# Linear attention and a gated MLP in one kernel: other transposes for two output pairs, other PSUM banks in the tail, other engine orders

## The chip, the cores and the metric

One core of one Trainium2 chip. The metric is the device time of one launch in microseconds (us). TensorE is called PE here, VectorE DVE, ScalarE ACT, GpSimd POOL, SyncE SP.

## The reference

```python
h  = x + A(layernorm(x))          # x: 1 x 2048 x 448, bf16
h2 = h + B(layernorm(h))          # the output

def A(x):                         # linear attention, 16 heads of 28
    q, k, v = split(x @ wqkv)     # wqkv: 448 x 1344
    phi = lambda t: where(t > 0, t + 1, exp(t)) + 1e-6
    pq, pk = phi(q), phi(k)
    kv, z = sum_s pk[s,d] v[s,e], sum_s pk[s,d]
    o = (pq @ kv) / (pq . z + 1e-6)
    return o @ wo                 # wo: 448 x 448

def B(x):                         # gated MLP, 448 -> 1792 -> 448
    return (gelu_tanh(x @ w_gate) * (x @ w_up)) @ w_down
```

## The kernel before

The 2048 rows are 16 tiles of 128 (`t`), worked in eight pairs (`p`) where it helps. The stages:

1. *LayerNorm and projections.* Each tile is normalised and transposed into `xnT` (tiles 0 to 3 by PE transposes `tr0_t`, `tr1_t`; the others by crossbar DMA `xT_t` on SP). `k_t` and `q_t` multiply it with the K and Q weights: four matmuls over 448 rows, the last one over the 64 tail rows and 64 rows of zeros. `pt..._t` adds K's share to a 448 x 448 sum that is kept in four PSUM banks. The weights' tail rows of K and Q come in one DMA on ACT (`dw0_t`).
2. *The attention matrix.* The sums are evicted (`evpA`, `evpD`, `z1`, `z0`), multiplied with the V weights (`kv`), masked (`kvm`, `kvd`) and multiplied with `wo`: `w2_0` to `w2_3`. A second copy of `w2` with its row halves swapped, `w2s`, is made by two DMAs (`dws0`, `dws1`).
3. *Attention output by pairs* (`a2_pair`). DVE, POOL and ACT make the normalised queries `pqn` (`cq`, `aq`, `t1`, `dr`, `rd`, `pn`). They are transposed into `pqnT` and multiplied with `w2`. Pair 0 has two zero-padded tiles of 512 columns, transposed on PE (`tro_0`, `tro_1`, evicted by ACT), and its output `out1_t` is four 128-row matmuls for a tile. All other pairs are 896 columns without padding, transposed by one crossbar DMA (`oT_p`); their tiles are multiplied at the same time in the two 64-row halves of the array, `outA_p` and `outB_p`, where part B waits for part A. Then the residual (`hr`), the LayerNorm statistics (`bnst2`, `bnag2`), `hn` on POOL (`nhP`; for pair 0 on DVE), its copy behind itself (`wrap`), and the transpose into `hnT` (`trh` on PE for pair 0, `hT_t` by crossbar DMA else).
4. *MLP.* `gu2_v` and `gu4_v` (56 groups `v`; 0 to 6 are tiles 0 and 1, 7 to 13 tiles 2 and 3, then 14 for each four tiles) make gate and up in the two row halves at once. ACT makes the gelu in two halves (`ge0_v`, `ge1_v`), DVE the product (`hm0_v`, `hm1_v`). Groups of even and of odd number have two PSUM banks each, so group v waits for the products of group v - 2.
5. *Down and output.* `downA_p`, `downB_p` for pairs 0 to 6 in 64-row halves; tiles 14 and 15 in 128-row mode: `down448_14`, and `down224_15` twice, for the two halves of the columns. Eviction with residual is `fo`, the output DMA `do_t`, all of them on SP.

Every operation is a task with buffers that it reads and writes; waits on semaphores come from these. The order of the tasks on each of the five engines is written out by hand as lists of numbers (`ORDERS`), and each engine works its own list strictly in order; `HOLD` only chooses which of several waits stands first.

Of the kernel before, what the change touches and what calls it, by code (L numbers as in the profile page):

```python
# [228 lines left out]
def bass_sequential_preLN__linear_attn_block__glu_gated_geglu__prompt_kernel(  # L229
# [19 lines left out]
    with es:  # L249
# [95 lines left out]
        def dma(q, out_ap, in_ap, w, name, r=(), after=()):  # L345
            t_ = G.add(q, lambda e: e.dma_start(out_ap, in_ap), r=r, w=w, name=name, kind="dma", after=list(after) + last[q])  # L346
# [210 lines left out]
        def a2_pair(p):  # L557
            a = 2 * p
            i2 = p % 2
            pst = D if p else 512  # L560
# [32 lines left out]
            if p == 0:  # L593
                for n in range(2):
                    def ftro(e, n=n):
                        ins = None
                        for g in range(NG):
                            ins = e.transpose(psb[:, BK_TO[n], g * 128:(g + 1) * 128], pqn[:, i2, n * 512 + g * 128:n * 512 + (g + 1) * 128], ident[:])
                        return ins
# [84 lines left out]
        def b2_pair(p):  # L684
            a = 2 * p
            sl = [slice((t % HR) * 128, (t % HR + 1) * 128) for t in (a, a + 1)]
            parts = []
            for half in range(2):
                def fdp(e, W, half=half):
                    ins = None  # L690
                    for j in range(NJ):
                        W(j)
                        for n in range(2):
                            rows = (A_, B_)[(n + half) % 2]
                            ins = e.matmul(ps[:, BK_O[n], 0:D], hh[rows, j, sl[n]], wd_sb[rows, j, :], start=(half == 0 and j == 0), stop=(half == 1 and j == NJ - 1))  # L695
                    return ins
                parts.append(G.add("pe", fdp, r=[(b_ar[j][t % HR], j if j >= NJ - 2 else 0) for j in range(NJ) for t in (a, a + 1)] + [b_wd],
                                   w=[b_ps[b_] for b_ in BK_O], name="down%s_%d" % ("AB"[half], p), mw=True, sync=parts[-1:]))
            for n, t in enumerate((a, a + 1)):
# [1 line left out]
                op("dve", lambda e, t=t, psO=psO: e.tensor_tensor(x_sb[:, t, :], psO, x_sb[:, t, :], ALU.add), [b_ps[BK_O[n]], b_x[t]], [b_x[t]], "fo448_%d" % t)  # L701
                G.add("sp", lambda e, t=t: e.dma_start(outv[:, t, :], x_sb[:, t, :]), r=[b_x[t]], name="do_%d" % t, kind="dma_out")
# [114 lines left out]
```

## Time and profile before

| | us |
|---|---|
| median of 3 runs (lowest to highest) | 191.09 (191.04 to 191.24) |
| the profiled execution's own time | 190.7 |
| its span, with a granted PE clock of 0.999 | 188.9 |
| busy: PE, DVE, ACT, POOL | 184.3, 127.8, 76.4, 50.0 |
| first K projection starts | 6.32 |
| last sum of `pt` leaves PE | 34.59 |
| first gate/up group starts | 50.50 |
| first pair of the last down parts starts | 175.12 |
| last output DMA is issued | 186.89 |

Times of rows are from the span's start. A row of the timeline has start, duration, engine, line, operation, output<-inputs, shapes and the number of merged instructions; brackets hold the idle time before it and who ended it. A row of groups has a count behind `x`. Rows whose engine ends in q (SPq, ACTq) are DMA issues.

### The profile page before, as it was taken

Reading aid. Unit: us, or ns where it says so; the run is one execution under the profiler, and the core shown is the slowest. Engines: PE = TensorE matmul, PEld = TensorE weight load, DVE = VectorE, ACT = ScalarE, POOL = GpSimd, SP = SyncE. Lnnn points to the kernel's source line nnn. Section 1 sums busy time; section 2 is a strip of 40 time slices with the busy share of each in tenths; the row PEclk is TensorE's granted clock in tenths of the full one; section 3 lists DMA queues with packets and bytes.
Section 4 is the critical chain, followed back from the end, with each engine's and each line's share of the span. In section 5 each row is a group of like instructions: output and inputs, shape, how many; then the busy total and the mean of one; then the engine's idle time right before and its main releaser. Section 6 shows DMA issues by size and latency. Waiting matters only on the chain.

```text
span 188.9 us, 4454 instructions
## 1 busy us (share of the span) xinstructions
PE 184.3 (98%) x1813; PEld 108.4 (57%) x1813; DVE 127.8 (68%) x328; ACT 76.4 (40%) x220; POOL 50.0 (26%) x91
## 2 busy tenths in 40 slices
PE   7799999999999999999999999999999999999994
PEld 7355555555688788965555555545545545454643
DVE  4999859999899998786796762562744343345232
ACT  3778752799963231432234222222142222324100
POOL 5067920604405686023614000207100000000000
PEclk9999999999999999999999999999999999999999
DMA  5985558999493525920005720000095000001025
GB/s 174 384 226 80 94 113 174 222 217 189 61 323 64 97 52 112 88 52 0 0 3 97 144 53 0 0 3 2 8 153 87 3 0 24 3 0 49 3 83 184
DMA packets 34996, 17.11 MB, mean 91 GB/s; under 512 B 26848, under 2 KB 33568, under 8 KB 34976
## 3 DMA queue, kind: packets, MB, share of 16 engines
q1 hardware_dynamic: 34352, 16.26, 41.4%
q10 hardware_dynamic: 624, 0.57, 0.9%
q8 instruction: 14, 0.23, 0.5%
q14 instruction: 6, 0.05, 0.1%
HBM read 8.26 MB, written 1.84 MB: 53 GB/s over the span
## 4 chain that ended last, share of the span: by engine, by line
PE 93%; DMA 3%; DVE 2%; ACTq 0%; issue 0%
PE ps L727 38%; PE ps L695 19%; PE ps L468 12%; PE ps L725 9%; PE ps L487 6%; DMA wqk_sb<-in_A_wqkv_dram 3%; PE ps L677 3%; PE ps L626 3%; PE ps L627 2%; PE ps L616 1%; PE ps L546 1%; PE ps L526 1%; ACTq L346 0%; PE ps L653 0%; DVE den L571 0%; DVE pt_sb L515 0%
## 5 line engine op out<-in xcount | busy, mean ns | idle before, releaser
L727 PE MATMUL ps<-hnT,wgu_sb 64*128 64x512 bf16 (+1 forms) x490 | 88.8, 333 | 0.0
L725 PE MATMUL ps<-hnT,wgu_sb 64*128 64x512 bf16 (+1 forms) x490 | 88.6, 333 | 0.0
L745 ACT ACTIVATE gl<-ps 128x256 bf16<-128x256 f32 x112 | 36.6, 383 | 85.3 <-PE ps L725 84.4
L747 DVE TENSOR_TENSOR hh<-ps,gl 128x256 bf16<-128x256 f32 x112 | 42.1, 416 | 41.5 <-ACT gl L745 41.4
L727 PEld LDWEIGHTS ps<-hnT,wgu_sb 64*128 64x128 bf16 x490 | 45.2, 94 | 32.9 <-DVE hh L747 3.4
L725 PEld LDWEIGHTS ps<-hnT,wgu_sb 64*128 64x128 bf16 x490 | 45.5, 94 | 2.6
L695 PE MATMUL ps<-wd_sb,hh 64*128 64x448 bf16 x392 | 41.7, 349 | 0.0
L695 PEld LDWEIGHTS ps<-wd_sb,hh 64*128 64x128 bf16 x392 | 22.7, 94 | 14.9 <-issue 0.2
L468 PE MATMUL ps<-wqk_sb,xnT 128*128 128x448 bf16 x128 | 27.5, 353 | 0.2 <-DMA wqk_sb<-in_A_wqkv_dram 0.2
L412 DVE BATCH_NORM_STATS2 st<-x_sb 128x6 f32<-128x448 bf16 x32 | 19.2, 612 | 1.8 <-DMA x_sb<-in_A_x_dram 1.7
L468 PEld LDWEIGHTS ps<-wqk_sb,xnT 128*128 128x128 bf16 x128 | 12.2, 98 | 11.7 <-DMA wqk_sb<-in_A_wqkv_dram 0.5
L584 POOL TENSOR_TENSOR t<-pq,zbc 128x448 f32<-128x448 bf16 x12 | 12.3, 1042 | 23.7 <-DVE pq L582 22.0
L487 PE MATMUL ps<-pk,xnn 128*128 128x448 bf16 x64 | 13.9, 352 | 0.0
L701 DVE TENSOR_TENSOR x_sb<-ps,x_sb 128x448 bf16<-128x448 f32 x14 | 8.5, 617 | 5.4 <-PE ps L695 5.4
L626 PE MATMUL ps<-w,pqnT 64*128 64x448 bf16 x49 | 11.5, 349 | 0.1
L424 POOL TENSOR_SCALAR ln<-mv 128x2 f32<-128x2 f32 x7 | 2.0, 290 | 35.2 <-DVE mv L413 35.0
L479 ACT ACTIVATE e<-ps 128x448 bf16<-128x448 f32 x16 | 8.5, 539 | 6.1 <-PE ps L468 5.9
L627 PE MATMUL ps<-pt_sb,pqnT 64*128 64x448 bf16 x42 | 10.2, 350 | 0.0
L632 DVE TENSOR_TENSOR x_sb<-ps,x_sb 128x448 bf16<-128x448 f32 x16 | 9.6, 616 | 0.7 <-PE ps L627 0.6
L661 POOL TENSOR_SCALAR hn<-x_sb,nm,rs 128x448 bf16<-128x448 bf16 x14 | 9.9, 719 | 0.4
L481 DVE SCALAR_TENSOR_TENSOR pk<-ps,e 128x448 bf16<-128x448 f32 x16 | 9.8, 617 | 0.1
L487 PEld LDWEIGHTS ps<-pk,xnn 128*128 128x128 bf16 x64 | 6.3, 98 | 5.8 <-DVE pk L481 0.3
(83 smaller groups left out, 158.4 us busy)
## 6 DMA issues: line engine op xcount, KB each, us to landing
out_dram<-x_sb SPq DMA_DIRECT2D x15, 112.0 KB, 1.8
wd_sb<-in_B_w_down_dram SPq DMA_DIRECT2D x1, 1568.0 KB, 8.3
x_sb<-in_A_x_dram SPq DMA_DIRECT2D x3, 448.0 KB, 6.5
wgu_sb<-in_B_w_gate_dram SPq DMA_DIRECT2D x1, 896.0 KB, 12.2
wgu_sb<-in_B_w_up_dram SPq DMA_DIRECT2D x1, 896.0 KB, 16.5
wgu_sb<-in_B_w_gate_dram SPq DMA_DIRECT2D x1, 672.0 KB, 6.1
wgu_sb<-in_B_w_up_dram SPq DMA_DIRECT2D x1, 672.0 KB, 8.6
wo_sb<-in_A_wo_dram SPq DMA_DIRECT2D x1, 392.0 KB, 8.2
```

Source lines behind the costliest of these rows:

```text
L412: op("dve", lambda e: e.bn_stats(st[:, t, :], src_ap), [b_src], [b_st[t]], "bnst%s_%d" % (tag, t))
L468: ins = e.matmul(ps[:, bk, 0:D], xnT[:, t, k, :], wqk_sb[:, k, c0:c0 + D], start=(k == 0), stop=(k == 3))
L487: ins = e.matmul(ps[:, BK_PT[c], 0:D], xnn[:, t % XN_R, c * 128:(c + 1) * 128], pk[:, ip, :], start=(t == 0), stop=(t == T - 1))
L584: op("pool", lambda e, n=n: e.tensor_tensor(t1[:, n, :], pq[:, a + n, :], zbc[:, :], ALU.mult), [b_pq[a + n]] + b_z, [b_t1[n]], "t1p_%d" % ...
L626: e.matmul(ps[:, BK_OUT[0], 0:D], pqnT[ra, i2, sg // 2, :], w2[ra, sg // 2, :], start=(sg == 0), stop=(sg == 5))
L627: ins = e.matmul(ps[:, BK_OUT[1], 0:D], pqnT[rb, i2, 3 + (sg + 1) // 2, :], (w2 if sg == 6 else w2s)[rb, sg // 2, :], start=(sg == 0), sto ...
L661: op("pool", lambda e, t=t, sh=sh: e.tensor_scalar(hn[:, sh, 0:D], x_sb[:, t, :], nm2[:, t:t + 1], rs2[:, t:t + 1], ALU.add, ALU.mult), [b ...
L695: ins = e.matmul(ps[:, BK_O[n], 0:D], hh[rows, j, sl[n]], wd_sb[rows, j, :], start=(half == 0 and j == 0), stop=(half == 1 and j == NJ - 1))
L725: first = e.matmul(psG[:, jj * N:(jj + 1) * N], wgu_sb[A_, k, j * 128:(j + 1) * 128], hnT[A_, ka_, c0:c0 + N], start=(k == 0), stop=(k == ...
L727: ins = e.matmul(psU[:, jj * N:(jj + 1) * N], wgu_sb[B_, k, j * 128:(j + 1) * 128], hnT[B_, kb_, c0:c0 + N], start=(k == 0), stop=(k == NK ...
L745: G.add("act", lambda e, gi=gi, cs_=cs_, psG=psG: e.activation(gl[:, gi, cs_], psG[:, cs_], AF.Gelu_apprx_tanh), r=[b_ps[BK_G[i]]], w=[b_g ...
L747: op("dve", lambda e, dst=dst, srcU=srcU, srcL=srcL: e.tensor_tensor(dst, srcU, srcL, ALU.mult), [b_ps[BK_U[i]], b_glh], [b_ar[j_][t % HR] ...
```

## The change

- Pair 0's output is transposed by one crossbar DMA (`oT_0`, eight blocks) in place of `tro` on PE and two ACT evictions. It waits for both tiles.
- Pair 1 is padded like pair 0 and its output made by `out1_2`, `out1_3` in 128-row mode.
- Pair 6's down has banks 4 and 5, so that it can run while pair 5's banks 2 and 3 are still used; the last two tiles take banks 2, 3 and 0.
- The tail rows of the K weights stay on ACT (448 of the 896 columns), those of Q come on SP (`dw1_t`), each with its own buffer, so that a projection waits for its own.
- All five orders and `HOLD` are new.

```diff
-        tx1 = dma("act", wqk_sb[A_, 3, :], A_wqkv[384:448, 0:2 * D], [b_wt], "dw0_t")
+        tx1 = dma_w1("act", wqk_sb, D, 2 * D, b_wk, "dw0_t")
         dma_w3("sp", wqk_sb, 0, D, b_wq, "dw1")
+        dma_w1("sp", wqk_sb, 0, D, b_wq, "dw1_t")
...
-            return [(b_xnT[t][0], 0), (b_xnT[t][1], 2), (b[0], 0), (b_wt, 3), (b_wpad[0], 3)]
+            return [(b_xnT[t][0], 0), (b_xnT[t][1], 2), (b[0], 0), (b[1], 3), (b_wpad[0], 3)]
...
-            pst = D if p else 512
+            pst = D if p > 1 else 512
...
-            if p == 0:
-                for n in range(2):
-                    def ftro(e, n=n): ...
-                    G.add("pe", ftro, r=[b_pqn[i2][n], b_ident], w=[b_ps[BK_TO[n]]], name="tro_%d" % n)
-                    op("act", ..., [b_ps[BK_TO[n]]], [b_pqnT[i2][n]], "evo_%d" % n)
-            else:
-                G.add("sp", lambda e, i2=i2: e.dma_start_transpose(pqnT[:, i2, 0:NK, :], pqn[:, i2, 0:2 * D]),
+            nb = 8 if p < 2 else NK
+            G.add("sp", lambda e, i2=i2: e.dma_start_transpose(pqnT[:, i2, 0:nb, :], pqn[:, i2, 0:nb * 128]),
                       r=b_pqn[i2], w=b_pqnT[i2], name="oT_%d" % p, kind="dma")
...
-            if p == 0:
+            if p < 2:
                 for n in range(2):
                     def fout(e, W, n=n): ...
...
-        BK_L = {T - 2: (4,), T - 1: (5, 2)}
+        BK_L = {T - 2: (2,), T - 1: (3, 0)}
+        BK_O6 = (4, 5)
...
+            bko = BK_O6 if p == 6 else BK_O
```

The parts of the orders that matter below, by the tasks' names (- before, + after):

```diff
 PE, start
- tr0_0 tr1_0 tr0_1 tr1_1 k_0 tr0_2 tr1_2 k_1 q_0 tr0_3 tr1_3 k_2 k_3 pt4_0 q_1 pt4_1 pt4_2 q_2 k_4
+ tr1_0 tr0_0 k_0 tr1_1 tr0_1 q_0 tr0_2 tr0_3 tr1_2 k_1 tr1_3 k_2 pt4_0 k_3 q_1 pt4_1 q_2 pt4_2 q_3 k_4
 DVE, start
- bnst1_1 bnag1_1 normD_0 bnst1_2 normD_1 bnag1_2 bnst1_3 evxD_0
+ bnst1_1 bnag1_1 normD_0 bnst1_3 bnst1_2 bnag1_3 evxD_0 bnag1_2 normD_1
 PE, from the last sums to the first MLP groups
- pt3_15 q_5 q_4 kv q_7 q_8 w2_2 w2_0 w2_1 q_9 w2_3 tro_1 tro_0 q_6 out1_1 out1_0 q_10 q_11 q_13 q_12 q_14 q_15 trh_1 trh_0 outA_1 outB_1
- gu2_0 gu2_1 outA_2 gu2_2 gu2_3 outB_2 gu2_4 gu2_5 outA_3 gu2_6 outB_3 downA_0 gu2_8 gu2_7 downB_0 gu2_9 gu2_10 outA_4 gu2_11 outB_4 gu2_12 gu2_13 gu4_14
+ pt3_15 q_9 q_5 q_6 q_7 kv q_8 q_10 w2_1 w2_0 w2_3 w2_2 q_11 out1_0 out1_1 q_15 q_13 q_14 q_12 out1_3 trh_0 trh_1 out1_2
+ gu2_0 gu2_1 gu2_2 gu2_3 gu2_4 outA_2 gu2_5 outB_2 gu2_6 downA_0 outA_3 gu2_8 outB_3 gu2_7 downB_0 gu2_9 gu2_10 gu2_11 outA_4 gu2_12 outB_4 gu2_13 gu4_14
 DVE, the first pair's queries
- dr_0 evpD_2 rd_0 dr_1 dr_2 kvm rd_2 kvd dr_3 rd_1 pn_0 rd_3 pn_1
+ dr_0 evpD_2 dr_1 rd_0 evpD_3 dr_2 rd_1 pn_0 pn_1 dr_3 rd_2 cqP_2 kvm pn_2 rd_3 kvd pn_3
 ACT, at the table load tbl2
- evhA_0 eq_13 rq_14 rq_13 tbl2 ge0_0 ge1_0
+ evhA_0 eq_12 rq_12 tbl2 ge1_0 ge0_0
 DVE, first MLP groups of the order after
+ hm1_0 hm0_0 hr_2 hm1_1 hm0_1 bnag2_3 bnst2_2 bnag2_2 cqP_4 hm0_2 hm1_2 drP_3 wrap_3 hm1_3 rdP_3 hm0_3 wrap_2 hm0_4 hm1_4 pnP_3 cqP_5 hm0_5 aqP_4 hm1_5 hr_4 hm1_6 hr_5 hm0_6
+ drP_4 aqP_5 rdP_4 bnst2_4 bnst2_5 pnP_4 bnag2_5 bnag2_4 hr_6 hr_7 cqP_6 bnst2_7 bnag2_7 bnst2_6 hm1_7 hm0_7 hm1_8 bnag2_6 hm0_8 wrap_4 drP_5 wrap_5 wrap_6 hm0_9 hm1_9
 POOL, pairs 2 and 3 of the order after
+ vpe2_4 pow2_4 negm2_4 nhP_4 t1p_10 nhP_5 vpe2_6 negm2_6 pow2_6 nhP_6 nhP_7
 SP, after the last xT
- dwg0 dwu0 dwg1 dwu1 dws0 dws1 oT_1 oT_2 dwd oT_3 hT_3 hT_2
+ dwg0 dwu0 dwg1 oT_0 oT_1 dwu1 dws0 dws1 oT_2 dwd hT_3 hT_2 oT_3
 PE, end
- downB_5 gu4_53 gu4_52 gu4_55 gu4_54 downA_6 down224_15 downB_6 down448_14 down224_15
+ gu4_53 downA_5 gu4_54 gu4_55 downA_6 downB_5 downB_6 down224_15 down448_14 down224_15
 SP, end
- do_1 hT_13 do_5 do_8 do_11 do_9 do_15 do_4 do_0 do_12 do_3 do_6 do_2 do_13 do_10 do_14 do_7 do_15
+ do_0 do_1 do_10 do_7 do_8 do_13 do_6 do_2 do_5 do_9 do_11 do_4 do_3 do_12 do_14 do_15 do_15
```

`dw1_t` stands on SP behind `dw1` and ahead of the DMAs of x from tile 4 on; `oT_0` stands behind three of the four gate/up weight DMAs and ahead of the fourth. `outA_3` and `outB_3` both stand behind `downA_0` now.

More of the change, by code (lines that the diff above doesn't have):

```diff
@@ L15 @@
 ORDERS = (
[33 rows of a table removed]
[33 rows of a table added]
 )
 HOLD = {
-    65: (35,), 140: (139,), 164: (163,), 213: (212,), 215: (214,), 322: (301,), 325: (323,), 430: (339,), 703:
-    (563,), 734: (733,), 780: (671,), 838: (835,), 848: (845,),
+    37: (34,), 66: (36,), 141: (140,), 232: (231,), 305: (302,), 360: (357,), 562: (427,), 696: (494,), 714:
+    (711,), 861: (860,),
 }
@@ L312, in bass_sequential_preLN__linear_attn_block__glu_gated_geglu__prompt_kernel @@
         b_wpad = bufs("wpad", 2)
-        b_wt = _Buf("wt")
         b_wo, b_wg, b_wu, b_wd = _Buf("wo"), bufs("wg", 2), bufs("wu", 2), _Buf("wd")
@@ L391, in bass_sequential_preLN__linear_attn_block__glu_gated_geglu__prompt_kernel @@
         op("pool", lambda e: e.memset(pt_sb[:, 3, :], 0.0), [], [b_pt[3]], "ptpad")
-        op("pool", lambda e: e.memset(pqn[:, 0, :].rearrange("p (n c) -> p n c", n=2)[:, :, D:512], 0.0), [], b_pqn[0], "pqnpad")
+        op("pool", lambda e: e.memset(pqn[:, :, :].rearrange("p b (n c) -> p (b n) c", n=2)[:, :, D:512], 0.0), [], b_pqn[0] + b_pqn[1], "pqnpad")
         op("pool", lambda e: e.memset(kvz[:, GW:15 * GW], 0.0), [], [b_kvm], "kvzpad")
@@ L592, in a2_pair @@
                    b_pq[b2] + b_rd[i:i + 2], b_pqn[i2], "pnP_%d" % p)
-            if p == 0:
-                for n in range(2):
[L595 to L599, printed above, removed]
-                    G.add("pe", ftro, r=[b_pqn[i2][n], b_ident], w=[b_ps[BK_TO[n]]], name="tro_%d" % n)
-                    op("act", lambda e, n=n: e.activation(pqnT[:, i2, 4 * n:4 * n + 4, :], psb[:, BK_TO[n], 0:512].rearrange("p (g t) -> p g t", g=NG), AF.Identity),
-                       [b_ps[BK_TO[n]]], [b_pqnT[i2][n]], "evo_%d" % n)
-            else:
-                G.add("sp", lambda e, i2=i2: e.dma_start_transpose(pqnT[:, i2, 0:NK, :], pqn[:, i2, 0:2 * D]),
+            nb = 8 if p < 2 else NK
+            G.add("sp", lambda e, i2=i2: e.dma_start_transpose(pqnT[:, i2, 0:nb, :], pqn[:, i2, 0:nb * 128]),
                       r=b_pqn[i2], w=b_pqnT[i2], name="oT_%d" % p, kind="dma")
@@ L694, in fdp @@
                             rows = (A_, B_)[(n + half) % 2]
-                            ins = e.matmul(ps[:, BK_O[n], 0:D], hh[rows, j, sl[n]], wd_sb[rows, j, :], start=(half == 0 and j == 0), stop=(half == 1 and j == NJ - 1))
+                            ins = e.matmul(ps[:, bko[n], 0:D], hh[rows, j, sl[n]], wd_sb[rows, j, :], start=(half == 0 and j == 0), stop=(half == 1 and j == NJ - 1))
                     return ins
                 parts.append(G.add("pe", fdp, r=[(b_ar[j][t % HR], j if j >= NJ - 2 else 0) for j in range(NJ) for t in (a, a + 1)] + [b_wd],
-                                   w=[b_ps[b_] for b_ in BK_O], name="down%s_%d" % ("AB"[half], p), mw=True, sync=parts[-1:]))
+                                   w=[b_ps[b_] for b_ in bko], name="down%s_%d" % ("AB"[half], p), mw=True, sync=parts[-1:]))
             for n, t in enumerate((a, a + 1)):
-                psO = ps[:, BK_O[n], 0:D]
-                op("dve", lambda e, t=t, psO=psO: e.tensor_tensor(x_sb[:, t, :], psO, x_sb[:, t, :], ALU.add), [b_ps[BK_O[n]], b_x[t]], [b_x[t]], "fo448_%d" % t)
+                psO = ps[:, bko[n], 0:D]
+                op("dve", lambda e, t=t, psO=psO: e.tensor_tensor(x_sb[:, t, :], psO, x_sb[:, t, :], ALU.add), [b_ps[bko[n]], b_x[t]], [b_x[t]], "fo448_%d" % t)
                 G.add("sp", lambda e, t=t: e.dma_start(outv[:, t, :], x_sb[:, t, :]), r=[b_x[t]], name="do_%d" % t, kind="dma_out")
```

66 rows, old and new, of the table ORDERS are left out of this document.

## The prediction

> **What bounds the kernel now.** I read the page first: TensorE (PE) works for nearly the whole span.
>
> ```profile
> PE 184.3 (98%) x1813; PEld 108.4 (57%) x1813; DVE 127.8 (68%) x328; ACT 76.4 (40%) x220; POOL 50.0 (26%) x91
> ```
>
> Nothing can become faster except by removing matmul time or one of the few places where PE waits. I looked for those in the timeline of PE, by start times: pipelined matmuls overlap, so the step is the distance of two starts.
>
> ```profile
> 6.32 0.92 PE L468 MATMUL ps<-wqk_sb,xnT 128*128 128x448 bf16 x3
> 7.46 0.36 PE L468 MATMUL ps<-wqk_sb,xnT 128*128 128x448 bf16 x1 [0.23 <-DMA wqk_sb<-in_A_wqkv_dram]
> ...
> 34.59 1.68 PE L468 MATMUL ps<-wqk_sb,xnT 128*128 128x448 bf16 x8
> 36.32 1.03 PE L526 MATMUL ps<-pt_sb,wv_sb 128*112 128x112 bf16 x16
> ...
> 40.80 0.61 PE L598 MATMUL ps<-ident,pqn 128*128 128x128 bf16 x8
> 41.24 0.92 PE L468 MATMUL ps<-wqk_sb,xnT 128*128 128x448 bf16 x4
> 42.00 1.68 PE L616 MATMUL ps<-w,pqnT 128*128 128x448 bf16 x8
> 43.51 4.70 PE L468 MATMUL ps<-wqk_sb,xnT 128*128 128x448 bf16 x24
> ...
> 48.93 0.36 PE L626 MATMUL ps<-w,pqnT 64*128 64x448 bf16 x1
> ...
> 49.92 0.36 PE L626 MATMUL ps<-w,pqnT 64*128 64x448 bf16 x1
> ...
> 50.50 0.27 PE L727 MATMUL ps<-hnT,wgu_sb 64*128 64x256 bf16 x1
> ```
>
> A 448-column matmul steps at (43.51 - 42.00) / 8 = 0.189 us. Three waits show: the first K tile's last matmul, held for its weights' tail until 7.46; 0.22 before `kv` (34.59 + 8 x 0.189 = 36.10, next start 36.32); and in the second pair's output, where eight matmuls (four steps, 0.76) should end at 49.69 but part B starts at 49.92, 0.23 late, since it waits for part A. From 50.50 PE has no wait worth naming until the last tiles, whose rows come with the tail below.
>
> **The change part by part.** Gains first.
>
> *Start.* The K tail becomes half as large and the Q tail a transfer of its own. At best K0's last matmul follows the third (6.32 + 3 x 0.189 = 6.89) and gains about 0.55. But the new DVE order puts the statistics of tiles 3 and 2 ahead of tile 1's normalisation, and Q0, now third on PE, needs its own tail. The reverse bound is one more wait of the same size. I take -0.15, nearer to nothing, as the same eight transposes and four projections still wait for the same DVE operations; range -0.5 to +0.5.
>
> *kv.* Four Q tiles (3.03 us) instead of two now cover the evictions ahead of it: -0.22. If they came later than two more tiles, the 0.22 would stay.
>
> *First pair's output.* Eight transposes leave PE: 41.24 - 40.80 = -0.44. The two evictions leave ACT. The crossbar transfer is hidden behind `kv`, two Q tiles, `w2` and one more Q tile; the price if it isn't is a rival below.
>
> *Second pair.* 50.50 - 48.93 = 1.57 becomes eight 128-row steps, 1.51: -0.06. It no longer needs the swapped copy `w2s`, so nothing of those two DMAs is on its path.
>
> These sum to -0.87. The K half has a price of +0.1: the order puts Q3 ahead of K4, on the bank that Q1's two ACT evictions free, and the last crossbar transposes of x come just when K14 wants them (0 to +0.4).
>
> Now the waits that the new orders make. *The gelu table.* These rows are ACT, DVE and PE behind the first tile's transposed LayerNorm.
>
> ```profile
> 49.21 0.95 ACT L657 ACTIVATE hnT<-ps 128x896 bf16<-128x896 bf16 x1
> 50.43 1.04 ACT L496 ACTIVATE pq<-ps 128x448 bf16<-128x448 f32 x2
> 51.48 1.28 ACT L756 ACT_TABLE_LOAD   x1
> 52.78 0.66 ACT L745 ACTIVATE gl<-ps 128x256 bf16<-128x256 f32 x2
> ...
> 53.47 0.76 DVE L747 TENSOR_TENSOR hh<-ps,gl 128x256 bf16<-128x256 f32 x2
> ...
> 54.32 0.27 PE L727 MATMUL ps<-hnT,wgu_sb 64*128 64x256 bf16 x1
> ```
>
> From `evhA_0` at 49.21 to the end of the second product at 54.23 are 5.02 us, and `gu2_2`, which reuses `gu2_0`'s banks, starts at 54.32. It doesn't wait only because `outA_2` (0.76) stands before it: 50.50 to 54.32 is two gate/up steps of 1.53 and those 0.76. After the change `gu2_0` to `gu2_4` run back to back. The ACT chain loses one eviction (-0.42) and takes the product halves in the order in which gelu makes them (-0.28): 4.32. PE can be at `gu2_2` 0.95 + 0.07 + 3.06 = 4.08 after `evhA_0` starts. So PE waits about +0.3 (0 to +0.7 with the chain as long as now). The Trainium skill, page "ScalarE: Activation LUTs", section "What ACT_TABLE_LOAD costs", gives 1283 ns for the load and 1380 ns more for a drain; the trace agrees with the load alone (1.28, and the gelu starts 0.02 after it). By the page's full figure this wait would be 1.4 longer; the measurement decides.
>
> *The LayerNorm of tiles 2 to 7 in DVE's order.* POOL makes `hn`, DVE copies it behind itself (`wrap`), in order, among gate/up products.
>
> ```profile
> 56.83 0.24 DVE L413 BATCH_NORM_AGGREGATE mv<-st 128x2 f32<-128x6 f32 x2
> 57.17 0.23 POOL L424 TENSOR_SCALAR ln<-mv 128x2 f32<-128x2 f32 x1 [4.91 <-DVE mv L413]
> 58.69 1.42 POOL L661 TENSOR_SCALAR hn<-x_sb,nm,rs 128x448 bf16<-128x448 bf16 x2
> 59.88 0.36 DVE L663 COPY hn<-hn 128x448 bf16<-128x448 bf16 x1
> ...
> 64.89 0.23 POOL L424 TENSOR_SCALAR ln<-mv 128x2 f32<-128x2 f32 x1
> 66.54 1.42 POOL L661 TENSOR_SCALAR hn<-x_sb,nm,rs 128x448 bf16<-128x448 bf16 x2
> ...
> 67.06 1.07 DVE L585 TENSOR_REDUCE den<-t 128x32 f32<-128x896 f32 x1
> 69.28 1.08 DVE L589 TENSOR_TENSOR pqn<-pq,rd 128x896 bf16<-128x896 bf16 x1
> ```
>
> From the aggregates' end (57.07) to the end of the first normalised tile (58.69 + 0.72 = 59.41) are 2.34 us; DVE now does seven other operations meanwhile and the copy at 59.88 waits for nothing. In the new order stand only `cqP_4`, two products and `drP_3`, some 2.0 with their own waits, then `wrap_3`. From `gu2_2`'s start: the aggregate, behind `hr_2`, two products and a statistics, is done at +1.85, the tile ready at +4.2, `wrap_3` to +4.5, and behind it `hm1_3`, `rdP_3`, `hm0_3` (0.34 + 0.27 + 0.41) to +5.55. `gu2_5` reuses that bank and PE would be there at 3 x 1.53 + 0.76 = +5.35. Wait: +0.2 (0 to +0.7).
>
> The same at pair 3, where both its output parts now stand behind `downA_0`. Counted from the end of `gu2_6`: the first product can start at +0.6, and DVE then needs two products and `hr_5` (1.2), `drP_4`, `pnP_4` (2.0), `aqP_5`, `rdP_4`, two statistics (1.9) and the aggregates (0.24), to +5.9. POOL needs 66.54 - 64.89 = 1.65 to begin `nhP_4`, then `nhP_4`, `t1p_10`, `nhP_5` (0.7 + 1.04 + 0.7), the next pair's three small operations (58.69 - 57.17 = 1.52) and `nhP_6` (0.72): +12.3. Then `wrap_6`, `hm0_9`, `hm1_9` (0.26 + 0.34 + 0.41): +13.3. PE reaches `gu2_11`, which needs that bank, after two down parts (28 matmuls in 14 steps, 2.65 each), `outA_3` and `outB_3` (1.32) and four gate/up steps (6.12): +12.74. Wait: +0.6 (0 to +1.1).
>
> *The tail.*
>
> ```profile
> 175.12 3.02 PE L695 MATMUL ps<-wd_sb,hh 64*128 64x448 bf16 x28
> 178.07 1.51 PE L677 MATMUL ps<-wd_sb,hh 128*128 128x224 bf16 x14
> 179.52 2.82 PE L695 MATMUL ps<-wd_sb,hh 64*128 64x448 bf16 x28
> 182.28 4.16 PE L677 MATMUL ps<-wd_sb,hh 128*128 128x448 bf16 x28
> ...
> 182.38 1.15 DVE L701 TENSOR_TENSOR x_sb<-ps,x_sb 128x448 bf16<-128x448 f32 x2 [2.37 <-PE ps L695]
> 186.47 0.39 DVE L681 TENSOR_TENSOR x_sb<-ps,x_sb 128x224 bf16<-128x224 f32 x1 [0.72 <-PE ps L677]
> ...
> 183.03 2.79 SPq L702 DMA_DIRECT2D out_dram<-x_sb  x6
> ...
> 186.89 0.41 SPq L682 DMA_DIRECT2D out_dram<-x_sb  x1
> ```
>
> Own banks let pair 6's down run beside pair 5's: `downA_6`, `downB_5`, `downB_6`, then all 128-row work, one change of row mode instead of three. Each costs about 0.1 (179.52 to 182.28 is 2.76 for work of 2.65): PE gains 0.2. But SP's queue is in order too. It now has `do_13` early, and behind it `do_6 2 5 9 11 4 3 12 14` and both halves of tile 15: eleven issues. `do_13` needs pair 6's second eviction, 183.53 in the row above, 1.25 after the last down pair. Issues follow each other at (186.89 - 183.03) / 8 = 0.48. So the last one goes 1.28 + 11 x 0.48 = 6.56 after the down pairs, while its data are ready at 1.35 + 4.16 + 0.03 + 0.39 + 0.03 = 5.96. Now eight issues follow `do_12` and the last starts 0.03 after its data: no slack. Against now the end moves by -0.2 + 0.6 = +0.4 (from -0.2 if issues could go faster than any here, to +0.5).
>
> **Sum.** -0.87 + 0.1 + 0.3 + 0.2 + 0.6 + 0.4 = +0.7; the steps left over (POOL's copies that collide, next part) can only add, so I take +0.8: profiled 190.7 becomes 191.5, and the runs' median, 191.09, becomes 191.9. The profiled time is 0.4 below the median; the difference is what carries over. All from `gu4_14` to `downA_6` I cost at nothing: a gate/up step of 1.51 then covers two products and the pairs' DVE work is spread over 75 us.
>
> **Rivals.**
>
> *The copies collide with POOL (slower still).* One POOL row and the DVE row beside it:
>
> ```profile
> 72.83 1.05 POOL L584 TENSOR_TENSOR t<-pq,zbc 128x448 f32<-128x448 bf16 x1
> 72.98 1.03 DVE L663 COPY hn<-hn 128x448 bf16<-128x448 bf16 x1
> ```
>
> A `wrap` started 0.15 into a POOL operation took 1.03 and ended 0.13 after it; the one at 59.88, inside the second `hn` tile (59.39 to 60.11), 0.36. The new `wrap_3` and `wrap_6` are released just as POOL starts its next `hn` tile, so each could last 0.7 instead of 0.26: +0.5 twice, 192.9. That is the Trainium skill's rule in "SBUF — State Buffer", section "Who interferes with whom": copies of this kind and POOL share a port pair, and whoever comes first holds it for its whole instruction. The two rows agree with it. Against: POOL's next operation may not have the pair yet.
>
> *The DVE waits don't bind (faster).* Decides: `wrap_3` and `wrap_6` find their tiles ready, as every `wrap` does now, and the table load is covered. Then -0.87 + 0.1 + 0.4 = -0.4: 190.7.
>
> *Half of them bind (no change).* Only the 0.6 at `gu2_11`, or the other two: +0.1 to +0.2, 191.2.
>
> *The first pair's transpose lands late.*
>
> ```profile
> 39.62 0.56 DVE L575 TENSOR_TENSOR pqn<-pq,rd 128x448 bf16<-128x448 bf16 x1
> ...
> 29.04 0.63 SPq L346 DMA_DIRECT2D wgu_sb<-in_B_w_gate_dram  x1
> wgu_sb<-in_B_w_gate_dram SPq DMA_DIRECT2D x1, 896.0 KB, 12.2
> pqnT<-pqn SPq DMA_TRANSPOSE x3, 3.0
> ```
>
> Its source, ready at 40.2 now, stands about 1.1 earlier in the new DVE order (ahead of a sum, two reciprocals and both mask operations), so at 39.1, and lands at 42.1 by the median of 3.0. It also queues behind the third gate/up weight transfer, down at 29.04 + 12.2 = 41.2. The first reader is due at 34.6 + 0.8 (Q4, moved ahead) + 7.5 (seven Q tiles, `kv`, `w2`) - 0.15 = 42.7. If the transpose came at 43.2 everything behind would shift by 0.5: 192.4.
>
> **How the numbers follow.** Forecast (191.9) 0.42; collisions (192.9) 0.23; late transpose (192.4) 0.08; no change (191.2) 0.15; faster (190.7) 0.12. The range leaves out the last and the far bounds of collisions: 190.8 to 193.2. About 0.2%, 0.4 us, is what a measurement of this kernel can tell from no change. Faster 0.12; same 0.16; slower 0.72.
>
> **What would show it.** PE's rows: no L598, `kv` without a wait, a gap ahead of the third and sixth gate/up groups and one near 76; `wrap` rows of 0.26 or 0.7; on SP a run of issues without a pause to the end, the last over 0.5 us after the last eviction. A PE timeline without gaps between 50 and 80, or a last issue right behind its eviction, would prove me wrong.

## The result, and the profile after

| | before | after |
|---|---|---|
| median (lowest to highest), us | 191.09 (191.04 to 191.56), 5 runs | 193.09 (192.77 to 193.84), 5 runs |
| ratio, 95% interval | | 1.0106 [1.0081, 1.0131] |
| profiled execution: its time / its span | 190.7 / 188.9 | 192.77 / 190.7 |
| last sum of `pt` leaves PE | 34.59 | 35.82 (now with Q4, 0.76, ahead of it) |
| first gate/up group starts | 50.50 | 50.34 |
| `gu4_14` starts | 81.17 | 82.42 |
| `downA_6` starts | 175.12 | 173.75 (now with `downB_5`, 2.65, behind it) |
| last output DMA is issued | 186.89 | 188.62 |

The change makes the kernel 2.0 us slower; 0.8 was forecast. By the stages of the table, up to `gu2_0` it gains 0.16, from there to `gu4_14` it loses 1.41, to `downA_6` 0.04 (2.65 added back), to the last issue 0.45: 1.74 of span. The other 0.3 lies outside the span: time minus span is 1.77 before and 2.09 after.

PE's timeline after, in the K half and up to the first gate/up group (start, length, merged matmuls behind `x`):

```profile
6.33 1.11 PE L469 MATMUL ps<-wqk_sb,xnT 128*128 128x448 bf16 x4 [0.48 <-ACT xnT L448]
...
17.10 0.92 PE L469 MATMUL ps<-wqk_sb,xnT 128*128 128x448 bf16 x4
18.11 0.93 PE L488 MATMUL ps<-pk,xnn 128*128 128x448 bf16 x4
...
20.39 0.92 PE L488 MATMUL ps<-pk,xnn 128*128 128x448 bf16 x4
21.35 0.93 PE L469 MATMUL ps<-wqk_sb,xnT 128*128 128x448 bf16 x4
...
35.82 3.19 PE L469 MATMUL ps<-wqk_sb,xnT 128*128 128x448 bf16 x16
38.85 0.99 PE L527 MATMUL ps<-pt_sb,wv_sb 128*112 128x112 bf16 x16
...
42.51 0.92 PE L469 MATMUL ps<-wqk_sb,xnT 128*128 128x448 bf16 x4
43.35 1.67 PE L607 MATMUL ps<-w,pqnT 128*128 128x448 bf16 x8
...
49.46 0.92 PE L607 MATMUL ps<-w,pqnT 128*128 128x448 bf16 x4
50.34 0.28 PE L717 MATMUL ps<-hnT,wgu_sb 64*128 64x256 bf16 x1
```

K0's four matmuls run through (before, the last of them was held until 7.46); `kv` starts 16 steps of 0.189 behind the Q tiles, without its wait; no `tro` is left between 41 and 43. Those gains are there. But four matmuls take 0.757, so 17.10 to 18.11 holds a wait of 0.25 and 20.39 to 21.35 one of 0.20, which the K half did not have before.

Two places in the MLP's first groups, DVE, POOL and PE:

```profile
57.81 0.30 DVE L654 COPY hn<-hn 128x448 bf16<-128x448 bf16 x1 [0.28 <-POOL hn L652]
...
73.87 1.50 POOL L652 TENSOR_SCALAR hn<-x_sb,nm,rs 128x448 bf16<-128x448 bf16 x2
74.61 0.33 DVE L654 COPY hn<-hn 128x448 bf16<-128x448 bf16 x1 [0.73 <-POOL hn L652]
...
76.07 0.61 DVE L583 TENSOR_TENSOR pq<-pq,eq 128x896 bf16<-128x896 bf16 x1
76.76 2.03 POOL L585 TENSOR_TENSOR t<-pq,zbc 128x448 f32<-128x448 bf16 x2 [1.39 <-DVE pq L583]
77.82 1.92 DVE L590 TENSOR_TENSOR pqn<-pq,rd 128x896 bf16<-128x896 bf16 x1
...
80.53 1.07 DVE L739 TENSOR_TENSOR hh<-ps,gl 128x256 bf16<-128x256 f32 x3
...
79.96 0.27 PE L717 MATMUL ps<-hnT,wgu_sb 64*128 64x256 bf16 x1
80.99 0.28 PE L719 MATMUL ps<-hnT,wgu_sb 64*128 64x256 bf16 x1 [0.77 <-DVE hh L739]
```

The product of the row at 77.82, in the kernel before:

```profile
79.21 1.09 DVE L589 TENSOR_TENSOR pqn<-pq,rd 128x896 bf16<-128x896 bf16 x1
```

The two L654 copies with a bracket are `wrap_3` and `wrap_6`. They do wait for POOL, as forecast, and are not stretched (0.30, 0.33). What is stretched is another instruction: the normalising product of pair 5, `pnP_5`, lasts 1.92. It starts just behind the first of POOL's two products of the row at 76.76 (`t1p_13`) and lies beside the second (`t1p_12`, 77.75 to 78.79); before, POOL did nothing beside it and it lasted 1.09. Behind it, `hm0_11` of the group at 80.53 frees the bank that the second matmul of `gu2_13` needs, and PE stands from 79.96 to 80.99: 0.94 more than a step.

The tail after, PE, DVE and SP's queue (before: last issue 0.03 behind its data):

```profile
173.75 8.31 PE L687 MATMUL ps<-wd_sb,hh 64*128 64x448 bf16 x84
181.99 5.50 PE L668 MATMUL ps<-wd_sb,hh 128*128 128x224 bf16 x42
...
182.11 1.16 DVE L693 TENSOR_TENSOR x_sb<-ps,x_sb 128x448 bf16<-128x448 f32 x2 [1.49 <-PE ps L687]
187.54 0.39 DVE L672 TENSOR_TENSOR x_sb<-ps,x_sb 128x224 bf16<-128x224 f32 x1 [0.42 <-PE ps L668]
...
180.11 7.47 SPq L694 DMA_DIRECT2D out_dram<-x_sb  x12
187.62 1.45 SPq L673 DMA_DIRECT2D out_dram<-x_sb  x3
```

The last sum ends at 187.93; the last of the three issues from 187.62 to 189.07 starts at 188.62, 0.69 later. `do_13` goes at 183.29, right behind its eviction (182.11 + 1.16 = 183.27), and eleven issues follow at 0.48 with nothing idle between them.

### The profile page after: what moved, and what is told of

The parts are those of the page before. It is cut to its first block, busy times and chain, and to the rows that moved or that the text cites. A ratio compares the mean times of both kernels' runs of the same rounds, so it can differ in the third digit from the quotient of the medians.

```text
span 190.7 us, 4421 instructions
## 1 busy us (share of the span) xinstructions
PE 185.1 (97%) x1799; PEld 108.3 (57%) x1799; DVE 129.9 (68%) x328; ACT 75.2 (39%) x218; POOL 49.7 (26%) x91
## 4 chain that ended last, share of the span: by engine, by line
PE 91%; DVE 6%; ACT 0%; issue 0%; POOL 0%; POOLq 0%
PE ps L719 38%; PE ps L687 19%; PE ps L469 9%; PE ps L717 9%; PE ps L488 5%; PE ps L668 3%; DVE st L413 2%; PE ps L407 2%; PE ps L617 2%; PE ps L607 2%; PE ps L618 2%; DVE pk L482 1%; PE ps L547 1%; DVE e L481 1%; PE ps L527 0%; PE ps L644 0%
## 5 line engine op out<-in xcount | busy, mean ns | idle before, releaser
L739 DVE TENSOR_TENSOR hh<-ps,gl 128x256 bf16<-128x256 f32 x112 | 42.6, 416 | 35.8 <-ACT gl L737 35.5
L687 PE MATMUL ps<-wd_sb,hh 64*128 64x448 bf16 x392 | 41.1, 349 | 0.0
L652 POOL TENSOR_SCALAR hn<-x_sb,nm,rs 128x448 bf16<-128x448 bf16 x14 | 10.4, 754 | 0.7
L617 PE MATMUL ps<-w,pqnT 64*128 64x448 bf16 x42 | 9.9, 349 | 0.0
L453 POOL TENSOR_SCALAR xnn<-x_sb,nm,rs 128x448 bf16<-128x448 bf16 x12 | 9.0, 748 | 2.0 <-ACT rs L422 1.8
```

The source lines that it names most:

```text
L617: e.matmul(ps[:, BK_OUT[0], 0:D], pqnT[ra, i2, sg // 2, :], w2[ra, sg // 2, :], start=(sg == 0), stop=(sg == 5))
L652: op("pool", lambda e, t=t, sh=sh: e.tensor_scalar(hn[:, sh, 0:D], x_sb[:, t, :], nm2[:, t:t + 1], rs2[:, t:t + 1], ALU.add, ALU.mult), [b ...
L687: ins = e.matmul(ps[:, bko[n], 0:D], hh[rows, j, sl[n]], wd_sb[rows, j, :], start=(half == 0 and j == 0), stop=(half == 1 and j == NJ - 1))
L739: op("dve", lambda e, dst=dst, srcU=srcU, srcL=srcL: e.tensor_tensor(dst, srcU, srcL, ALU.mult), [b_ps[BK_U[i]], b_glh], [b_ar[j_][t % HR] ...
```

## The experiments

All runs were compared with the kernel before on the same chip; the changed kernel itself was not run again beside them, so what a move gains on it is read from the paths in the profiles. "Before" and "after" in a heading say which kernel was edited; orders are given by task names.

**1. Tile 13's output DMA behind tile 12's (after).**

```diff
 SP, end
- do_8 do_13 do_6 do_2 do_5 do_9 do_11 do_4 do_3 do_12 do_14 do_15 do_15
+ do_8 do_6 do_2 do_5 do_9 do_11 do_4 do_3 do_12 do_13 do_14 do_15 do_15
```

> The changed kernel with one output DMA moved in SP's order: do_13 behind do_12 instead of ahead of do_6. Theory (SP's order sets the end): the last issue, 188.62 in the changed kernel's profile and 0.69 after its data, comes right behind them, at about 187.96 from the same PE end; profile 0.65 shorter (about 190.0 span), median about 192.4. Rival (the output DMAs themselves, not their order, limit the tail): the last issue stays 0.5 or more behind the last eviction, no change.

191.68, ratio 1.0044 [1.0029, 1.0059]. Its SP queue and its last sum:

```profile
180.16 5.78 SPq L701 DMA_DIRECT2D out_dram<-x_sb  x12
186.90 1.44 SPq L680 DMA_DIRECT2D out_dram<-x_sb  x3
...
187.59 0.39 DVE L679 TENSOR_TENSOR x_sb<-ps,x_sb 128x224 bf16<-128x224 f32 x1 [0.42 <-PE ps L675]
```

SP now has a pause (185.94 to 186.90), and its last issue starts at 188.01, 0.03 behind the last sum. The place of one DMA in the queue was the tail's whole loss of 0.66. The median is 0.7 below the theory's 192.4, more than the path shows (see experiment 5).

**2. `aqP_6` behind `pnP_5` (after).** `aqP_6` writes the operand of POOL's `t1p_12` and `t1p_13`; behind `pnP_5` it starts them later.

```diff
 DVE
- aqP_6 wrap_7 hm1_10 hm0_10 rdP_5 pnP_5 hm1_11 fo448_1
+ wrap_7 hm1_10 hm0_10 rdP_5 pnP_5 aqP_6 hm1_11 fo448_1
```

> The changed kernel with one DVE operation moved: aqP_6 behind pnP_5, so that POOL's t1p_13 and t1p_12, which read its result, can't run beside pnP_5. Theory (pnP_5 and POOL's product take turns): pnP_5 falls from 1.92 to about 1.08 us, the 0.94 wait of PE inside gu2_13 shrinks to 0.1 or 0.2, the profile is 0.8 shorter, median about 192.3. Rival (DVE is overbooked there whatever runs on POOL): pnP_5 falls, but PE still waits 0.5 or more in gu2_13 or the next two groups, gain under 0.3.

191.89, ratio 1.0054 [1.0039, 1.0069].

```profile
77.34 1.09 DVE L597 TENSOR_TENSOR pqn<-pq,rd 128x896 bf16<-128x896 bf16 x1
78.35 0.62 DVE L590 TENSOR_TENSOR pq<-pq,eq 128x896 bf16<-128x896 bf16 x1
...
79.05 2.04 POOL L592 TENSOR_TENSOR t<-pq,zbc 128x448 f32<-128x448 bf16 x2 [3.73 <-DVE pq L590]
```

Without POOL beside it the product takes 1.09 again, the wait at `gu2_13` falls from 0.94 to 0.22 and `gu4_14` starts at 81.66 instead of 82.42. DVE does the same work ahead of `hm0_11` as before the move, so its amount is not the cause.

**3. The same collision, made in the kernel before.**

```diff
 DVE (before): aqP_6 is moved ahead of hm0_11 and with it ahead of rdP_5 and pnP_5
```

> The kernel before with one DVE operation moved: aqP_6 ahead of hm0_11, so that POOL's t1p_12 and t1p_13 run beside pnP_5 there too. Theory (they take turns): pnP_5 grows from 1.09 to 1.6 or more, hm0_12 and hm1_12 come later and PE, without a wait there now, waits 0.4 to 0.9 at gu4_14; median 191.5 to 192.0. Rival (the order alone made the wait in the changed kernel, pnP_5's length doesn't matter): pnP_5 stays near 1.1 or the span moves by less than 0.2.

191.12, ratio 1.0015 [1.0005, 1.0025], less than expected.

```profile
78.46 2.04 POOL L594 TENSOR_TENSOR t<-pq,zbc 128x448 f32<-128x448 bf16 x2 [3.99 <-DVE pq L592]
79.82 1.63 DVE L599 TENSOR_TENSOR pqn<-pq,rd 128x896 bf16<-128x896 bf16 x1
```

The product overlaps POOL's second operation (79.46 to 80.50) for 0.68 and is 0.54 longer. So the collision is shown in both kernels, with and without; but here PE lost only 0.19, ahead of `gu4_14`, since in the order before no group waits that closely on what stands behind `pnP_5`. So the price of a collision depends on what follows it, and not on its length alone.

**4. The K half in the order before (after).**

```diff
 PE, DVE, ACT, POOL, SP: the tasks up to the last pt, ek, pk, norm and xT stand as before;
 Q4 (q_4, eq_4) stays ahead of K14; the split tail rows stay
```

> The changed kernel with the K half (all tasks up to the last pt sum) in the order of the kernel before on every engine; q_4 and its exponential stay ahead of k_14, the split tail rows stay. Theory (the new order of the K half costs, through pk_4 behind four statistics and x's transpose of tile 8 behind three ACT evictions): the waits at pt4_4 (0.26), k_8 (0.20) and q_3 (0.06) go, the last pt sum ends at 35.35 or earlier instead of 35.82, profile 0.4 to 0.6 shorter. Rival (the split tail or SP's extra DMA delays x): the waits stay or come elsewhere in the K half, and the last sum ends at 35.7 or later.

192.72, ratio 1.0094 [1.0076, 1.0113].

```profile
16.53 2.43 PE L477 MATMUL ps<-wqk_sb,xnT 128*128 128x448 bf16 x12
18.80 0.92 PE L496 MATMUL ps<-pk,xnn 128*128 128x448 bf16 x4
19.56 0.92 PE L477 MATMUL ps<-wqk_sb,xnT 128*128 128x448 bf16 x4
...
35.45 3.19 PE L477 MATMUL ps<-wqk_sb,xnT 128*128 128x448 bf16 x16
...
39.30 1.81 PE L477 MATMUL ps<-wqk_sb,xnT 128*128 128x448 bf16 x8
41.11 1.50 PE L555 MATMUL ps<-wo_sb,hh 112*128 112x448 bf16 x7
...
43.21 1.68 PE L615 MATMUL ps<-w,pqnT 128*128 128x448 bf16 x8
```

The steps in the K half are 0.76 for four matmuls again and it ends 0.37 earlier (35.45 against 35.82, between the theory's 35.35 and the rival's 35.7): PE lost 0.42 behind K2 in this profile, but from the step behind K2 to the last sum it takes 24.23 without Q4's 0.76, against 24.83 after and 24.21 before. The eight Q matmuls from 39.30, 1.51 of work, now take 1.81: Q10 waits 0.12 for ACT to free its bank, and `w2_1` 0.18 for the mask operation `kvm` on DVE. So `out1_0` starts only 0.14 earlier, although its transpose had landed at 42.78. At the first gate/up group (50.26) 0.08 are left: most of what the K half gives back is lost in the next stage.

**5. Both moves, 1 and 2 (after).**

> The changed kernel with both of the moves that each gained alone: tile 13's output DMA behind tile 12's on SP, and aqP_6 behind pnP_5 on DVE. Theory: the two prices are in series (0.65 us of issues at the end, 0.7 of pnP_5 beside POOL's products), so they add: pnP_5 1.09, wait before gu2_13 about 0.2, last issue within 0.1 of the last sum's end; last issue at 188.62 - 0.66 - 0.75 = 187.2, time 0.3 above the kernel before, ratio 1.001 (191.2). What is left above it is the K half and the first transpose. Rival: the prices overlap, or a later wait takes the slack up; then the time stays at 191.7, ratio 1.004.

191.49, ratio 1.0026 [1.0010, 1.0042] (12 runs). From the start of `gu2_0` to the last issue: after 138.28; with 1 alone 137.60; with 2 alone 137.54; with both 136.93; before 136.39. The gains, 0.68 and 0.74, nearly add: together 1.35 of the 1.89. The medians do not add: by their ratios to the kernel before, the moves gain 1.2 and 1.0 on the changed kernel, and together 1.5; why each alone gained more than its path shows is open. This profile started the MLP late (50.99), with 0.64 ahead of `out1_0`: the first transpose landed at 43.86. 0.54 stay; the waits left in that stretch are 0.18, 0.14, 0.13 and 0.21 at `gu2_5`, ahead of `outA_3`, at `gu2_11` and at `gu2_13`.

**6. The first transpose ahead of the third weight transfer as well (after).**

```diff
 SP
- dwg0 dwu0 dwg1 oT_0 oT_1 dwu1 dws0 dws1
+ dwg0 dwu0 oT_0 dwg1 oT_1 dwu1 dws0 dws1
```

> The same as e3_both, and the first pair's transposing DMA is issued ahead of the third gate/up weight transfer on SP, behind which it landed in every run of the changed kernel (0.9 after it), so that out1_0 had to wait 0.1 to 0.4. Theory: the transpose lands about 2.7 after its issue, 42.0 to 42.3, out1_0 starts at 42.9 without a wait, and everything behind gains 0.3 to 0.4: about 190.8, ratio 0.9995 (0.997 to 1.001). Rival: the third weight transfer now starts only when the normalised tiles are ready, 2 us later than the queue is free; the weights behind it then land late and the wait is found again at the gate/up steps or at downA_0 (its weights landed at 61.5, due near 62.3): same as e3_both or slower by up to 1.

192.32, ratio 1.0082 [1.0056, 1.0108]: the rival. SP's queue and PE:

```profile
39.09 1.25 SPq L602 DMA_TRANSPOSE pqnT<-pqn  x1
40.38 0.60 SPq L353 DMA_DIRECT2D wgu_sb<-in_B_w_gate_dram  x1
41.90 1.25 SPq L602 DMA_TRANSPOSE pqnT<-pqn  x1
...
wgu_sb<-in_B_w_gate_dram SPq DMA_DIRECT2D x1, 896.0 KB, 7.0
...
42.84 1.68 PE L614 MATMUL ps<-w,pqnT 128*128 128x448 bf16 x8
...
48.37 0.93 PE L614 MATMUL ps<-w,pqnT 128*128 128x448 bf16 x4 [0.82 <-DMA pqnT<-pqn]
...
66.37 0.36 PE L624 MATMUL ps<-w,pqnT 64*128 64x448 bf16 x1 [0.40 <-DMA pqnT<-pqn]
```

The first transpose lands at 42.15, 3.06 after its issue (43.22 in the profile after, 3.70), and `out1_0` starts at 42.84 without a wait. But the weight transfer issued at 40.38 lands at 47.34, and the second pair's transpose, issued behind it at 41.90, at 48.32: 0.82 of wait there. The weights of the down stage land at 62.52 instead of 61.52, still ahead of `downA_0` (63.06), but the transposes issued behind them are late too: pair 3's, `oT_3`, lands at 66.33 instead of 65.31, and `outA_3`, at 66.37, starts 0.67 late. One queue has to carry both, and the order only chooses who is late.

**7. The tail alone (before).** The evictions on DVE and the output DMAs on SP follow the new order.

```diff
 PE, end (before, with the new banks)
- downB_5 gu4_53 gu4_52 gu4_55 gu4_54 downA_6 down224_15 downB_6 down448_14 down224_15
+ gu4_53 gu4_52 gu4_55 gu4_54 downA_6 downB_5 downB_6 down224_15 down448_14 down224_15
```

> The kernel before with the tail alone: own banks for down pair six, downA_6 downB_5 downB_6 in a row and then all 128-row down steps, and the output DMAs of tiles 13 to 15 last on SP. Theory: two changes of row mode of 0.1 fewer, last issue right behind its data: 0.2 faster, 190.7, ratio 0.999. Rival: the banks give nothing, since the evictions of pair 6 now hold back another step: 1.000 or above. If the change's tail is dear for the own banks and not for the place of tile 13's DMA, this is 0.4 slower (1.002).

192.71, ratio 1.0092 [1.0071, 1.0112], and the theory's 0.2 is nevertheless there: from `downA_6` to the last issue 14.28, against 11.77 + 2.65 = 14.42 before. The loss is ahead of it:

```profile
167.57 0.39 PE L737 MATMUL ps<-hnT,wgu_sb 64*128 64x512 bf16 x1 [0.54 <-ACT gl L757]
168.69 0.39 PE L739 MATMUL ps<-hnT,wgu_sb 64*128 64x512 bf16 x1 [0.73 <-DVE hh L759]
```

Both rows are of one group, `gu4_53`, which reuses the banks of `gu4_51` and now stands directly behind it: its first gate matmul starts 0.91 late, behind the gelu, and its first up matmul another 0.92 late, behind the products. `downB_5`, which stood between the two groups, covered both (experiment 8 leaves it there and has no such wait). I had moved cover to the tail and costed that at nothing.

**8. Own banks, `downB_5` left in its place (before).** The eviction on DVE and the output DMAs on SP follow the new order.

```diff
 PE, end (before, with the new banks)
- downA_6 down224_15 downB_6 down448_14 down224_15
+ downA_6 downB_6 down224_15 down448_14 down224_15
```

> The kernel before with own banks for down pair six, but with downB_5 left where it was, among the last gate/up steps: only down224_15 moves behind downB_6, so that the row mode changes once at the end and not three times, and the output DMAs of tiles 12 to 15 come last on SP in the order of their sums. Theory: the waits ahead of downA_6 (0.31), down224_15 (0.11) and downB_6 (0.11) go, one change of 0.1 to 0.3 stays, the last issue follows its data: 0.2 to 0.4 faster, 190.75, ratio 0.998 to 0.999, and no wait in the last gate/up steps (in e8_before_tail 0.91 and 0.92 there, because downB_5 no longer lay between them). Rival: the banks themselves make the last gate/up steps wait, as in e8_before_tail: 1.005 or above.

190.89, ratio 0.9994 [0.9982, 1.0005]: no gain.

```profile
175.37 5.90 PE L707 MATMUL ps<-wd_sb,hh 64*128 64x448 bf16 x56
181.21 5.50 PE L688 MATMUL ps<-wd_sb,hh 128*128 128x224 bf16 x42
```

From `downA_6` to the last matmul are 11.08 (before 11.06). Before, PE loses 0.30 behind `downA_6`, 0.11 ahead of `downB_6` and 0.11 ahead of `down448_14`; here it loses 0.43 behind `downA_6`, where part B waits for part A, and 0.10 ahead of `down224_15`. PE's 0.2 came only where `downB_5` stands between the two parts: 13.49 after and 13.50 in experiment 7, against 13.71.

**9. The split tail rows alone (before).**

```diff
-        tx1 = dma("act", wqk_sb[A_, 3, :], A_wqkv[384:448, 0:2 * D], [b_wt], "dw0_t")
+        tx1 = dma_w1("act", wqk_sb, D, 2 * D, b_wk, "dw0_t")
         dma_w3("sp", wqk_sb, 0, D, b_wq, "dw1")
+        dma_w1("sp", wqk_sb, 0, D, b_wq, "dw1_t")
```

> The kernel before with the tail rows of the K and Q weights loaded apart (448 columns each, the K ones on ACT's queue, the Q ones on SP's behind the first three blocks) and nothing else. Theory: the K tail rows land about 0.4 earlier (7.42 to about 7.0) and the wait before the first K matmul (0.59 now) falls to 0.2 or 0.3; SP's transfers behind dw1 come 0.1 to 0.2 later. Gain 0.15 to 0.4 at the end of the K half; at the end 0 to 0.4: ratio 0.999 (0.998 to 1.000). Rival: the next limit (tiles' statistics and copies) takes it all: 1.000.

191.04, ratio 1.0003 [0.9988, 1.0017].

```profile
6.47 1.02 PE L478 MATMUL ps<-wqk_sb,xnT 128*128 128x448 bf16 x4
```

K0 runs through, as theory had it, and the median span falls from 189.3 to 189.05. But the time does not: it lies 1.99 above the span here and 1.79 before.

**10. Split and own banks together (before).**

> The same as e10_before_banks, and the K and Q tail rows loaded apart as in e9_before_split. Theory: if the split gains something, it adds: the wait before the first K matmul 0.1 to 0.3 instead of 0.6, ratio 0.9965 to 0.9985 (190.5). Rival: the split is worth nothing on the whole, as its 12 runs had it (1.0003): same as e10_before_banks.

190.97, ratio 0.9999 [0.9984, 1.0015]; the time lies 2.01 above the span. The parts that looked like gains do not make a version that beats the kernel before.

**11. Experiment 5 with the single transfer of the tail rows (after).**

> The same as e3_both, with the tail rows of K and Q loaded by one transfer again, as before (896 columns on ACT's queue). In all runs so far the time lies 1.8 above the span in kernels with the one transfer and 2.0 in those with two (e9_before_split 1.99, e11_before_banks_split 2.00, both steady). Theory: the split itself adds that 0.2 outside of the span and takes 0.2 off inside it, so here the wait before the first K matmul is 0.5 to 0.6, the span 189.6 (0.2 above e3_both's median of 189.4), the time 1.8 above the span, 191.4, ratio 1.002, nothing gained. Rival: the distance between time and span comes from the new orders; it stays at 2.0 to 2.2 here, the time is 191.7, ratio 1.0035. Second rival: without the split SP's transposes come earlier and the span falls too: 191.0, ratio 1.000.

191.45, ratio 1.0029 [1.0017, 1.0041], median span 189.5. The time lies 1.97 above the span, where my theory had 1.8: it is not the split as such. Counting the transfers on SP's queue gave another theory: 66 in before and experiments 3, 7 and 8 (1.72 to 1.86 in every run), 67 in 9, 10 and 11, 68 after and in the rest of its variants.

**12. One transfer more (before).**

```diff
-                G.add("sp", lambda e, t=t: e.dma_start(outv[:, t, :], x_sb[:, t, :]), ...)
+                for c0, c1 in ((0, D // 2), (D // 2, D)) if t == 0 else ((0, D),):
+                    G.add("sp", lambda e, ...: e.dma_start(outv[:, t, c0:c1], x_sb[:, t, c0:c1]), ...)
```

> The kernel before, with the output of tile 0 written by two DMAs of half its columns instead of one, in the same place on SP (followed there by a pause of 9.5 us). Nothing else. What it tells apart: the part of a run's time that lies outside the span was 1.78 in every run of four kernels with 66 transfers on SP, 1.93 to 2.05 in every run of the three with 67, and 1.7 to 2.2 in the changed kernel and its variants with 68. Theory (it goes by the number of transfers on SP's queue): span unchanged, 189.2, time 2.0 above it, ratio 1.001. Rival (it goes by something else that these kernels have in common, such as the split or the first transpose): 1.78, ratio 1.000.

191.08, ratio 1.0006 [0.9994, 1.0018]. Median span 189.1 against 189.2, and time minus span 1.96 (1.93 to 2.04 in 12 runs) against 1.80 (1.73 to 1.86 in 17). One harmless transfer moved the part outside the span by 0.16. The time itself, 191.08 against 191.00, can't be told from the kernel before.

## Why the prediction was right in direction and short in size

The span's path, step by step; forecast, then measured.

| step | forecast | measured | shown by |
|---|---|---|---|
| start | -0.15 | -0.15 | the first eight transposes and K0, Q0, K1, K2 end at 10.23 (10.38) |
| K half | +0.1 (0 to 0.4) | +0.62 | 35.82 against 34.59 + 0.76, less the start's -0.15; 4 |
| `kv`, first and second pair | -0.72 | -0.63 | rows 35.82 to 50.34 |
| gelu table, `gu2_2` | +0.3 | +0.05 | below |
| `wrap_3`, `gu2_5` | +0.2 | +0.13 | row 57.81 |
| `wrap_6`, `gu2_11` | +0.6 | +0.13 | row 74.61 |
| `oT_3`, ahead of `outA_3` | 0 | +0.14 | landing 65.31; 6 |
| `pnP_5`, `gu2_13` | 0 | +0.94 | 2, 3 |
| `gu4_14` to `downA_6` | 0 | +0.04 | |
| tail | +0.4 | +0.45 | 1 |
| outside the span | 0 | +0.3 | 12, for one of the two added transfers |

*Right.* The gains of the start, of `kv` and of `tro` came as worked out, and so did the tail with its mechanism: PE gained 0.22 (0.2 forecast), SP's queue lost 0.66 (0.6). My reason for PE's part was wrong, though: experiment 8 removed the same two changes of row mode and gained nothing. That the start agrees to the hundredth is luck: in the five profiles with the old K half and the single transfer of the tail rows, K2 ends anywhere from 10.38 to 10.81. That the sum came out near the range's upper end and not beyond it is partly luck too: the three waits that I forecast at the gate/up groups came to 0.31 instead of 1.1, and 0.94 at a group that I had costed at nothing took their place. The forecast of slower held, and the new order of DVE is still the largest cause, but through a collision and not through the waits that I added up.

*The waits for POOL's tiles and for the table* were there, but smaller. At `gu2_11` DVE's two products ended 13.04 after the end of `gu2_6` (75.61 against 62.57; forecast 13.3), and PE was there at 12.88 (forecast 12.74): a difference of two close numbers, 0.13 instead of 0.6. At `gu2_2` the ACT chain took 4.27 (4.32 forecast), but PE came 0.08 later than I had it. The mechanisms were right; the terms were over-sized, since each was the rest of two chains with an error of a few tenths each.

*The collision* was my rival, and its mechanism is true at another instruction. I priced the two `wrap` copies, which lasted 0.30 and 0.33, and not the product `pnP_5`, which the new order sets beside POOL's `t1p_12`. This is the term missing from the sum: 0.94, of which experiment 2 takes back 0.72. The row is 1.92 against 1.09. The Trainium skill, "SBUF — State Buffer", section "Who interferes with whom", says that a DVE instruction with both inputs in SBUF contends with a GpSimd instruction that reads SBUF. The rows agree: 0.83 longer for 0.97 beside POOL, and in experiment 3 0.54 longer for 0.68. The 0.7 that I had priced for a `wrap` copy does occur, at a place where no PE group waits for it:

```profile
57.77 0.85 POOL L652 TENSOR_SCALAR hn<-x_sb,nm,rs 128x448 bf16<-128x448 bf16 x1
57.81 0.30 DVE L654 COPY hn<-hn 128x448 bf16<-128x448 bf16 x1 [0.28 <-POOL hn L652]
...
137.15 0.71 POOL L652 TENSOR_SCALAR hn<-x_sb,nm,rs 128x448 bf16<-128x448 bf16 x1
137.25 0.74 DVE L654 COPY hn<-hn 128x448 bf16<-128x448 bf16 x1
```

`wrap_3` starts 0.05 into POOL's operation, and POOL's is the one that is stretched (0.85; alone 0.71); `wrap_14` starts 0.10 into it, and the copy is stretched (0.74; alone 0.26). `wrap_6` starts 0.05 into the next operation, like `wrap_3`. So my own argument against the rival, that POOL's next operation may not have the pair yet, is what held for the copies.

*The K half* was mis-sized: 0.62, beyond my bound of 0.4. The profile after is the dearest of six with this order; the others lie 0.35 to 0.53 above the kernel before. I had looked at Q3's bank and K14's transposes, where PE loses next to nothing (0.06, ahead of K4), and not at how soon behind a K tile its sum follows. `pt4_4`, the sum at 18.11, waits 0.26 for `pk_4` (0.25 or 0.26 in all six): in the new order it stands three steps behind the start of K4 (K4, `pt4_3`, K5), before it was five. The statistics that stand ahead of `pk_4` on DVE, which experiment 4's theory names, are not the reason: from the start of K4 to the end of `pk_4` are 2.47, against 2.83 before. The transpose of tile 8 lands at 21.30, just before K8 (0.20; at most 0.07 in the other five).

*The late transpose of the first pair*, my last rival, happened too: it landed at 43.22, where I had priced 43.2. It cost only 0.09, because PE was itself late by the K half. The K half and this transpose are not terms of a sum; the later one counts. `out1_0` starts 0.13 behind the landing after (43.22, 43.35), in experiment 2 (43.17, 43.30) and in 5 (43.86, 43.99); and in experiment 1 the K half ended 0.27 earlier than after, with `out1_0` at 43.41 all the same. Only where the transpose came early, in experiment 6, did it start before 43; in experiment 4, where it came at 42.78, the waits ahead of `w2_1` held `out1_0`.

*Pair 3's transpose* is a smaller term that I had put at nothing: `oT_3` now stands on SP behind `hT_3` and `hT_2`, and behind the weights of the down stage, which land at 61.52 (58.24 before). The three land at 63.80, 64.58 and 65.31, and `outA_3` starts at 65.36, 0.14 late.

*"The difference is what carries over"* failed: that step of the forecast was wrong. I took time minus span to be fixed. It went from 1.77 to 2.09, a sixth of the whole loss.

Not settled: the first pair's transpose alone was not tried on the kernel before, nor was the padding of the second pair. Of the 0.54 left in experiment 5 only the waits are named, not taken away.

## What to carry to other kernels

When an order is rewritten, look at what each long DVE instruction with two SBUF inputs will lie beside on POOL, and let the operation that releases POOL stand behind it; what it costs depends on the first PE group that needs what DVE does next. In an in-order DMA queue count the issues that stand behind the last one that has to wait for its data: one issue placed too early cost 0.66 here, and moving a transfer ahead of another only moved the wait. A step that covers a wait elsewhere is not free to move, however good its new place (0.2 gained in the tail, 1.8 lost ahead of it).
